# Attention and a gated MLP on one core: q and k of three pairs turned by one DMA transfer each, with two pairs' loads a unit sooner

## The chip, the core and the metric

The kernel runs on one core of a Trainium2 chip. A core has TensorE (PE, matmuls; its weight loads are listed as PEld), VectorE (DVE), ScalarE (ACT), GpSimd (POOL), and SyncE (SP), which here issues DMA transfers. They work side by side and wait for each other through semaphores; each takes its own instructions in order. Sixteen DMA engines move data for the core. The metric is the device time of one execution in microseconds; lower is better.

## The reference

```python
def _attn_ref(q, k, v):                    # q, k, v: (8, 12, 448, 64)
    scores = 1.0 / np.sqrt(64) * np.matmul(q, k.transpose(0, 1, 3, 2))
    m = np.max(scores, axis=-1, keepdims=True)
    e = np.exp(scores - m)
    attn = e / (np.sum(e, axis=-1, keepdims=True) + np.exp(-m) + 1e-09)
    return np.matmul(attn, v)
...
x = attn_out.transpose(0, 2, 1, 3).reshape(3584, 768)
h = x @ w_in                               # (3584, 2048)
sp = np.where(h > 20.0, h, np.log1p(np.exp(np.minimum(h, 20.0))))
return (h * np.tanh(sp)) @ w_out           # (3584, 768), float32
```

All inputs and the output are float32. The output has 3584 rows, 448 for each of eight batches.

## The kernel before, in words

**Pairs and units.** Two heads of a batch make a pair, so there are 48 pairs (p = 0 to 47), six per batch. Their head dimensions of 64 fill TensorE's 128 rows together. Three pairs make a unit (`UNIT_PAIRS`, line 16). Units 0 and 1 are a start-up loop of their own (lines 618 to 651); units 2 to 15 run in the loop of lines 653 to 746, and two more passes (16 and 17) finish the MLP.

**One pair.** q, k and v are loaded as float32 on 112 partitions by SP (`load_pair`, L121, issue at L128), cast to bfloat16 by GpSimd (`cast_pair`, L165, at L179 and L180, and `cast_v`, L188), and q and k are turned, so that the head dimension lies on the partitions. That is done by TensorE: eight transposes of 112 x 128 blocks per pair into a PSUM bank (`transpose_pair`, L208). `evac_qk` then brings them to SBUF: DVE scales q by 1/8 into a block-diagonal tile `qd` (L254, two instructions of 64 rows), and ACT copies k into `kT` (L262). Scores are matmuls of `qd` with `kT` (L311), four steps of up to two 128-row tiles per pair in three PSUM tiles. DVE takes the row maximum (L332), ACT the exponentials with their sums (L345), DVE the denominators (L365, L369), and from pair 12 on DVE divides before the next product (L414, seven per pair, `normalise`). The softmax weights of a pair, 28 blocks of 128 x 128, are turned by one DMA transposing transfer (L422, called a softmax turning here: `eT<-en`, issued by SP). Matmuls with v (`av_pair`, L462) give the turned attention output, which DVE casts into `xT` (L475).

**The MLP.** For a batch that is finished, `mm1_mish` multiplies `xT` by the first weights (L498, six matmuls for each of 16 slices) and ACT applies x * tanh(softplus(x)) (L504). `mm2_part` multiplies by the second weights (L551), DVE copies the result (L534) and SP stores it (L516).

**The order of a unit.** Everything is written out by hand, and each engine's queue has this order. A unit u has two parts. In the first, twelve steps (lines 664 to 717) run the exponentials of u's three pairs, the scores up to three steps ahead, the av products of the pairs of unit u - 1 (from unit 4 on), and mm2 chunks from `plan` as filler on PE. In steps 0, 3 and 6 (`LOAD_AT`, line 592) SP gets the q and k loads of the pair four further on (`LEAD`) and a v load, and GpSimd the casts of q and k three pairs further on. In the second part (lines 724 to 746), eight mm1 slices f = 0 to 7: denominators and the division of u's first pair at f = 0, of the others at f = 3 and 7, each followed by its softmax turning; at f = 1, 3 and 5 the transposes of one pair of the next unit on PE and `evac_qk`; at f = 4, 6 and 7 the first three scores of the next unit.

**Queues and buffers.** SP issues every load, turning and store in the order of the code, and waits in that order. `ld_pool` has three buffers each for q, k and v as loaded; the casted q and k have four buffers each, casted v twelve, `kT` three, `eT` three, and `qd` three (pair p uses p % 3).

Of the kernel before, what the change touches and what calls it, by code (L numbers as in the profile page):

```python
# [10 lines left out]
BF16 = mybir.dt.bfloat16  # L11
# [4 lines left out]
UNIT_PAIRS = 3  # L16
# [3 lines left out]
def kernel(  # L20
# [38 lines left out]
    singles = pool("singles", 1)  # L59
    ld_pool = pool("ld", 3)  # L60
    bf_pool = pool("bf", 4)
    qk_pool = pool("qk", 3)
    st_pool = pool("st", 5)
    hl_pool = pool("hl", 4)
    rb_pool = pool("rb", 2)
# [16 lines left out]
    w_in_sb = singles.tile([128, DM_T, d_ff], BF16)  # L82
    w_out_sb = singles.tile([128, FF_T, d_model], BF16)
    gT = singles.tile([128, FF_T, 2 * S], BF16)

    marks = singles.tile([1, 4, 16], BF16)
    N_EN = 5
# [74 lines left out]
            nc.gpsimd.dma_start(out=dst, in_=src.rearrange("(a p) c -> p a c", p=128))  # L162


    def cast_pair(p, with_v=True):  # L165
        if p >= N_PAIRS:
            return
        q_f, k_f, v_f = (loaded[p].get(nm) for nm in "qkv")
        q_bf = bf_pool.tile([SP_, NT, 2, D], BF16, tag="q_bf", name="q_bf")
        k_bf = bf_pool.tile([SP_, NT, 2, D], BF16, tag="k_bf", name="k_bf")  # L170
        v_bf = bf_pool.tile([SP_, 2, NT * D], BF16, tag="v_bf", name="v_bf", bufs=12)
        by_t = "p h (t d) -> p t h d"
        q_t, k_t = (t.rearrange(by_t, t=NT) for t in (q_f, k_f))
        if p == 0:
            nc.vector.tensor_copy(out=k_bf, in_=k_t)
            for half in (slice(0, NT // 2), slice(NT // 2, NT)):
                nc.vector.tensor_copy(out=q_bf[:, half], in_=q_t[:, half])
        else:
            nc.gpsimd.tensor_copy(out=q_bf, in_=q_t)  # L179
            nc.gpsimd.tensor_copy(out=k_bf, in_=k_t)  # L180
        casted[p] = (q_bf, k_bf, v_bf)
        if with_v:
            cast_v(p)

    def cast_v(p):
        if p >= N_PAIRS:
            return
        nc.gpsimd.tensor_copy(out=casted[p][2], in_=loaded.pop(p)["v"])  # L188

    def transpose_pair(p, bank=None):  # L190
        if p >= N_PAIRS:
            return
        q_bf, k_bf, _ = casted[p]
        if bank is None:
            ps = mo_take()
            ps_k = mo_take() if p == 0 else ps
        else:
            ps, ps_k = sc_tiles[2 - bank][:, 0, :], sc_tiles[2 - bank][:, 1, :]
        by_s = [
            t[:, :].bitcast(BF16).rearrange("p (s n) -> p s n", s=2)[:, s, :]  # L200
            for s, t in enumerate((ps, ps_k))
        ]
        by_2 = sc_tiles[2][:, 0, :].bitcast(BF16)
        srcs = list(enumerate((q_bf, k_bf)))
        for s, src in reversed(srcs) if p == 0 else srcs:
            for t in range(NT):
                to = by_2 if p == 0 and s == 0 and t >= NT // 2 else by_s[s]
                nc.tensor.transpose(  # L208
                    to[:, t * SP_ : (t + 1) * SP_],
                    src[:, t].rearrange("p h d -> p (h d)"),  # L210
                    ident[:SP_, :SP_],
                )
        own = [] if bank is not None else [ps, ps_k] if p == 0 else [ps]
        qkT[p] = (by_s, own)
# [6 lines left out]
    def evac_qk(p, act=False):  # L221
        if p >= N_PAIRS:
            return
        (q_ps, k_ps), own = qkT[p]
        mo_free.extend(own)
        q_reads = []
        qd = q_diag[p % 3]
        kT = qk_pool.tile([128, S], BF16, tag="kT", name="kT")
        if p < DIAG_FROM:
            qT = qd.rearrange("d i h r -> d (i h r)")[:, 0:S]  # L230
            qkT[p] = (qT, kT)
            if p == 0:
                nc.scalar.copy(kT, k_ps[:, 0:S])
                by_2 = sc_tiles[2][:, 0, :].bitcast(BF16)
                for ps, half in (q_ps, slice(0, S // 2)), (by_2, slice(S // 2, S)):
                    nc.vector.tensor_scalar(
                        out=qT[:, half], in0=ps[:, half], scalar1=SCALE, scalar2=None,
                        op0=ALU.mult,
                    )
                return  # L240
            if act:
                nc.scalar.mul(qT, q_ps[:, 0:S], SCALE)
            else:
                q_reads.append(nc.vector.tensor_scalar(
                    out=qT, in0=q_ps[:, 0:S], scalar1=SCALE, scalar2=None, op0=ALU.mult
                ))
        else:
            qkT[p] = (qd, kT)
            if p < DIAG_FROM + 3:
                nc.vector.memset(qd[0:64, :, 1, :], 0.0)  # L250
                nc.vector.memset(qd[64:128, :, 0, :], 0.0)
            for h in range(2):
                rows = slice(64 * h, 64 * h + 64)
                q_reads.append(nc.vector.tensor_scalar(  # L254
                    out=qd[rows, :, h, :],
                    in0=q_ps[rows, 0:S].rearrange("d (i r) -> d i r", i=QB),
                    scalar1=SCALE, scalar2=None, op0=ALU.mult,
                ))
        if own and not act:
            nc.vector.tensor_copy(out=kT, in_=k_ps[:, 0:S])  # L260
        else:
            k_read = nc.scalar.copy(kT, k_ps[:, 0:S])  # L262
            if not own:
                apart(k_read, *q_reads)
# [180 lines left out]
    def av_pair(p, bank=None, beside=None, half=None, hold=False):  # L445
        b, hp = p // HP, p % HP
        eT = att[p]["eT"]
        v_bf = casted[p][2]
        if b not in xT:
            xT[b] = xT_pool.tile([128, DM_T, S], BF16, tag="xT", name="xT")  # L450
        if half is not None:
            bank = free_half(half)
            mms = av_beside.setdefault(half * STEPS + STEPS - 1, [])
        av = mo_take() if bank is None else bank
        for j in range(NT):
            for h in range(2):
                if p >= DIAG_FROM:
                    by_h = eT[0:SP_, j, :].rearrange("c (i h r) -> c h i r", h=2, r=64)
                    e_h = by_h[:, h]
                else:  # L460
                    e_h = eT[0:SP_, j, h * S : (h + 1) * S]
                mm = nc.tensor.matmul(  # L462
                    av[h * 64 : (h + 1) * 64, 0:S],
                    lhsT=v_bf[:, h, j * D : (j + 1) * D],
                    rhs=e_h,
                    start=(j == 0), stop=(j == NT - 1),
                )
                if half is not None:
                    apart(mm, half_max[half])
                    mms.append(mm)  # L470

        def evac():
            to = xT[b][:, hp, :]
            if p >= LATE_DIV:
                read = nc.vector.tensor_copy(out=to, in_=av[:, 0:S])  # L475
            else:
                read = nc.vector.tensor_tensor(
                    out=to, in0=av[:, 0:S], in1=rb.pop(p), op=ALU.mult
                )
            if half in half_exp:  # L480
                apart(read, half_exp[half])
            elif beside is not None or half is not None:
                av_read[beside if half is None else half * STEPS + STEPS - 1] = read
            if bank is None:
                mo_free.append(av)

        if p in spread_copy:
            late.append(spread_copy.pop(p))
        (held if hold else late).append(evac)
        del att[p], casted[p], qkT[p]  # L490
# [100 lines left out]
    LEAD = UNIT_PAIRS + 1  # L591
    LOAD_AT = (0, 3, 6)
    HEAD = HP

    BY_PE = {HEAD - 1: 1, HEAD: -2, HEAD + 1: 2}
    AV_AT = {0: {1: 3, 5: 4, 8: 5}, 1: {1: 8, 4: 6, 8: 7}}
# [5 lines left out]
        load_pair(p, names)  # L602
    keep_busy(8, bank=sc_tiles[0][:, 0, :])
    for p in range(2):
        cast_pair(p, with_v=False)
        transpose_pair(p)
        if p == 0:
            evac_qk(p)
            scores_ahead(3)
    load_pair(3)  # L610
    cast_v(0)
    cast_pair(2, with_v=False)
    cast_v(1)
    cast_v(2)
    load_pair(4)


    for p in range(HEAD):
        for s in range(STEPS):
# [19 lines left out]
            if s == 2:  # L639
                if p >= 3:  # L640
                    spread_rden(p - 3)
                cast_pair(p + 3, with_v=p + 3 < HEAD)
            if s == 3:
                if p >= 3:
                    av_pair(p - 3, hold=True)
# [7 lines left out]
    for u in range(UNITS_PER_B, N_UNITS + 2 * UNITS_PER_B):  # L653
# [5 lines left out]
        p0 = u * UNIT_PAIRS  # L659
        if attn and u >= first_mm2:  # L660
            av_with.update({p0 + i: p0 + i - UNIT_PAIRS for i in range(UNIT_PAIRS)})
        end = min((u + 1) * UNIT_PAIRS, N_PAIRS) * STEPS

        for n in range(steps):
            pi, s = divmod(n, STEPS)
# [20 lines left out]
                fn()  # L686
                done += w
            scores_ahead(end)
            if n in LOAD_AT:
                at = p0 + LOAD_AT.index(n)  # L690
                load_pair(at + LEAD, "qk")
                load_pair(at + 1, "v")
                cast_pair(at + LEAD - 1, with_v=False)
                cast_v(at)
            for pe, n0 in BY_PE.items():
                j = n - n0
                first = 2 if pe == HEAD else 0
# [21 lines left out]

        moe = u < N_UNITS + UNITS_PER_B  # L720
        b, w = (u - UNITS_PER_B) // UNITS_PER_B, u % UNITS_PER_B
        nxt = p0 + UNIT_PAIRS
        todo = sorted(range(p0, nxt), key=lambda p: p in BY_PE)
        for f in range(FF_U):
            if moe:
# [53 lines left out]
```

## Time and profile before

| | |
|---|---|
| median of 3 runs | 480.28 us (480.0 to 481.32) |
| the profiled execution | 479.66 us |
| its span, first to last instruction | 477.9 us |
| granted TensorE clock, mean | 0.996 |
| instructions recorded | 9363 |
| HBM read, written | 45.61 MB, 11.01 MB |

The span is what the views of the profile divide up; the execution takes 1.8 us more than it. In a row of the stretches the numbers are the length in us, the busy us of each engine with its count of instructions, the granted clock, the mean busy share of the DMA engines and the GB/s that they moved. The share adds up the time of all packets, including their waiting, and so can pass 1. In a row of the groups, the part after the bar is the busy time, the mean ns of one instruction, and the engine's idle time just before them with what ended it. In a row of the order of time stand the start, the time to the last one's end, the engine and line, what is done, and how many instructions were merged into the row; for several DMA issues in one row the time includes waits between them.

### The profile page before, as it was taken

How to read it: one execution, taken by the hardware profiler on the slowest of the kernel's cores; microseconds unless marked ns; L12 is line 12 of the kernel's file. 1: busy time of each engine (PE TensorE's matmuls, PEld its weight loads, DVE VectorE, ACT ScalarE, POOL GpSimd, SP SyncE). 2: the span in 40 equal slices, each digit the busy share in tenths (PEclk: the TensorE clock that was granted, in tenths of full speed). 3: DMA queues.
4: the chain of work that ended last, by engine and by line, in shares of the span. 5: the costliest groups of instructions: out<-in, count | busy, mean ns of one | idle time of the engine just before them, and what ended most of it. 6: DMA issues, size and time to landing. Idle time of an engine off the chain costs nothing.

```text
span 477.9 us, 9363 instructions
## 1 busy us (share of the span) xinstructions
PE 458.8 (96%) x3291; PEld 257.8 (54%) x3291; DVE 358.7 (75%) x715; ACT 344.7 (72%) x907; POOL 103.8 (22%) x186
## 2 busy tenths in 40 slices
PE   6878999999999999999999999999999999999996
PEld 3344555555555565556555555555555555556563
DVE  5899849569898998889899979888898889421011
ACT  5998878788797868788787968687887978312300
POOL 3623536106031311304040312204040300000000
PEclk9999999999999999999999999999999999999999
DMA  8999999999999979898989999989989596961122
GB/s 215 227 224 213 234 222 183 185 212 233 195 301 207 261 149 214 211 198 227 192 229 171 267 156 260 198 192 231 190 220 198 173 181 156 156 142 34 34 63 71
DMA packets 204975, 91.09 MB, mean 191 GB/s; under 512 B 161792, under 2 KB 201472, under 8 KB 204928
## 3 DMA queue, kind: packets, MB, share of 16 engines
q1 hardware_dynamic: 197408, 84.18, 81.0%
q0 software_dynamic: 7488, 6.29, 8.8%
q8 instruction: 26, 0.43, 0.4%
q14 instruction: 21, 0.17, 0.1%
q10 hardware_dynamic: 32, 0.02, 0.0%
HBM read 45.61 MB, written 11.01 MB: 118 GB/s over the span
## 4 chain that ended last, share of the span: by engine, by line
PE 69%; DVE 8%; ACT 6%; issue 1%; DVEq 0%
PE mo L498 24%; PE mo L551 24%; PE sc L311 7%; ACT en L345 6%; PE sc L462 6%; DVE negm L332 5%; PE sc L498 3%; PE sc L208 3%; DVE en L414 1%; DVE xT L475 1%; PE mo L462 1%; DVE o_sb L534 1%; PE mo L272 0%; DVE eT L437 0%; ACT L345 0%
## 5 line engine op out<-in xcount | busy, mean ns | idle before, releaser
L345 ACT ACTIVATE en<-sc,negm 128x448 bf16<-128x448 f32 x336 | 208.7, 640 | 22.5 <-DVE negm L332 20.7
L332 DVE TENSOR_REDUCE negm<-sc 128x2 f32<-128x896 f32 x192 | 182.6, 970 | 39.6 <-PE sc L311 29.3
L551 PE MATMUL mo<-w_out_sb,gT 128*128 128x384 bf16 (+1 forms) x1024 | 166.8, 307 | 0.4 <-DVE rb L402 0.4
L498 PE MATMUL mo<-xT,w_in_sb 128*128 128x448 bf16 x672 | 141.9, 353 | 0.3 <-DVE xT L475 0.3
L551 PEld LDWEIGHTS <-gT 128*128 128x128 bf16 x1024 | 96.3, 98 | 56.0 <-issue 1.9
L504 ACT ACTIVATE gT<-mo 128x448 bf16<-128x448 f32 x112 | 59.3, 543 | 78.9 <-PE mo L498 78.6
L498 PEld LDWEIGHTS <-w_in_sb 128*128 128x128 bf16 x768 | 72.7, 98 | 63.4 <-issue 3.2
L179 POOL CAST q_bf<-q_f 112x512 bf16<-112x512 f32 x47 | 29.9, 635 | 222.1 <-DMA q_f<-in_q_dram 196.1
L414 DVE TENSOR_SCALAR en<-en,rden 128x448 bf16<-128x448 bf16 x252 | 74.2, 367 | 0.8
L311 PE MATMUL sc<-kT,qd 128*128 128x448 bf16 x252 | 71.6, 354 | 0.1
L345 ACT ACTIVATION_READ_ACCUMULATOR en<-sc,negm 128x1 f32 x336 | 71.0, 211 | 0.0
L534 DVE COPY o_sb<-mo 128x384 f32<-128x384 f32 (+1 forms) x64 | 31.8, 497 | 48.3 <-PE mo L551 48.1
L462 PE MATMUL sc<-eT,v_bf 112*64 112x448 bf16 x336 | 39.8, 357 | 1.4 <-ACT en L345 0.9
L311 PEld LDWEIGHTS <-qd 128*128 128x128 bf16 x252 | 24.4, 97 | 29.0 <-issue 12.9
L188 POOL CAST v_bf<-v_f 112x512 bf16<-112x512 f32 x48 | 29.9, 624 | 31.5 <-DMA v_f<-in_v_dram 31.4
L254 DVE TENSOR_SCALAR qd<-sc 64x448 bf16<-64x448 bf16 x72 | 27.7, 385 | 6.2 <-PE sc L208 5.4
L462 PEld LDWEIGHTS <-v_bf 112*64 112x64 bf16 x384 | 20.0, 109 | 20.0 <-issue 11.6
L180 POOL CAST k_bf<-k_f 112x512 bf16<-112x512 f32 x47 | 29.2, 622 | 6.1 <-DMA k_f<-in_k_dram 3.5
L262 ACT COPY kT<-sc 128x448 bf16<-128x448 bf16 x39 | 20.8, 534 | 0.6 <-PE sc L208 0.6
L498 PE MATMUL sc<-xT,w_in_sb 128*128 128x448 bf16 x96 | 20.8, 353 | 0.0
L475 DVE CAST xT<-sc 128x448 bf16<-128x448 f32 x33 | 20.3, 614 | 0.0
L208 PEld LDWEIGHTS <-q_bf 112*128 112x128 bf16 x192 | 13.7, 99 | 10.0 <-POOL q_bf L179 2.0
(61 smaller groups left out, 278.9 us busy)
## 6 DMA issues: line engine op xcount, KB each, us to landing
k_f<-in_k_dram SPq DMA_DIRECT2D x48, 224.0 KB, 5.2
q_f<-in_q_dram SPq DMA_DIRECT2D x48, 224.0 KB, 5.2
v_f<-in_v_dram SPq DMA_DIRECT2D x48, 224.0 KB, 5.5
w_in_sb<-in_moe_w_in_dram POOLq DMA_DIRECT2D x12, 256.0 KB, 8.7
w_out_sb<-in_moe_w_out_dram POOLq DMA_DIRECT2D x8, 384.0 KB, 10.1
out_dram<-o_sb SPq DMA_DIRECT2D x7, 336.0 KB, 3.7
out_dram<-o_sb SPq DMA_DIRECT2D x8, 288.0 KB, 4.8
out_dram<-o_sb SPq DMA_DIRECT2D x8, 240.0 KB, 3.4
```

Of the source, the lines that this page charges most:

```text
L179: nc.gpsimd.tensor_copy(out=q_bf, in_=q_t)
L180: nc.gpsimd.tensor_copy(out=k_bf, in_=k_t)
L188: nc.gpsimd.tensor_copy(out=casted[p][2], in_=loaded.pop(p)["v"])
L311: nc.tensor.matmul(sc[:, bk, 0:S], lhsT=qT[:, i].rearrange("d h r -> d (h r)"), rhs=kT, start=True, stop=True,)
L332: half_max[p] = nc.vector.tensor_reduce(out=negm, in_=sc[:, 0 : len(cols), 0:S], axis=AX.X, op=ALU.max, negate=True)
L345: e = nc.scalar.activation(out=st["en"][:, :, c, 0:SP_], in_=sc[:, bk, 0:S].rearrange("q (j c) -> q j c", j=NT), func=AF.Exp, bias=st["neg ...
L414: nc.vector.tensor_scalar(out=en[:, :, i, 0:SP_], in0=en[:, :, i, 0:SP_], scalar1=st["rden"][:, i : i + 1], scalar2=None, op0=ALU.mult,)
L462: mm = nc.tensor.matmul(av[h * 64 : (h + 1) * 64, 0:S], lhsT=v_bf[:, h, j * D : (j + 1) * D], rhs=e_h, start=(j == 0), stop=(j == NT - 1),)
L498: nc.tensor.matmul(h_ps[:, 0:S], lhsT=w_in_sb[:, dm, ff * 128 : (ff + 1) * 128], rhs=xT[b][:, dm, :], start=(dm == 0), stop=(dm == DM_T - 1),)
L504: nc.scalar.activation(out=gT[:, ff, b % 2 * S : b % 2 * S + S], in_=h_ps[:, 0:S], func=AF.Mish)
L534: nc.vector.tensor_copy(out=o_sb[:, cols.start : cols.start + n_dve], in_=st["o"][:, 0:n_dve])
L551: nc.tensor.matmul(st["o"][:, 0:n_cols], lhsT=gT[:, ff, i * 128 : (i + 1) * 128], rhs=w_out_sb[:, ff, cols], start=(ff == 0), stop=(ff == ...
```

## The change

From pair 18 on (`BY_DMA_FROM` = 2 * 6 + 2 * 3) PE no longer turns q and k. GpSimd casts q and k of three pairs into one tile each (`q_cast`, `k_cast`, 112 partitions x 12 blocks x 128 columns), and SP issues two DMA transposing transfers per unit: `k_cast` into `kT_all` (room for six pairs) and `q_cast` into `qT_all` (room for three). `evac_qk` scales q from `qT_all` on DVE as before and no longer copies k. For the pairs before 18 the PE path stays, with `kT` now inside `kT_all` and the casts inside `q_cast` and `k_cast`.

Where things stand changes too. The first turning (pairs 18 to 20) is issued in unit 5 at step 6, behind that step's loads. From unit 6 on all six casts of the next unit's q and k, the two turnings, the q and k loads of one pair and three v loads are put at step 0, behind the softmax turnings of the unit before; the q and k loads of two more pairs are put at step 11, one unit sooner than before, from unit 5 on. The buffers of casted v go from twelve to eight. From unit 5 on k is loaded and cast ahead of q.

In the built program PE has 480 rows fewer (240 transposes, each with its weight load), ACT 30 fewer; DVE has the same number. SP has 20 turnings more.

```diff
-    qk_pool = pool("qk", 3)
+    q_cast, k_cast = (
+        singles.tile([SP_, UNIT_PAIRS, NT, 2, D], BF16, tag=f"{nm}_cast", name=f"{nm}_cast")
+        for nm in "qk"
+    )
+    qT_all = singles.tile([128, UNIT_PAIRS, S], BF16)
+    kT_all = singles.tile([128, 2 * UNIT_PAIRS, S], BF16)
...
+    def turn_by_dma(p):
+        if not BY_DMA_FROM <= p < N_PAIRS:
             return
+        at = p % (2 * UNIT_PAIRS)
+        for to, src in (kT_all[:, at : at + UNIT_PAIRS], k_cast), (qT_all, q_cast):
+            nc.sync.dma_start_transpose(
+                out=to.rearrange("d g (t p) -> d (g t) p", t=NT),
+                in_=src.rearrange("p g t h d -> p (g t h d)"),
+            )
 
     def transpose_pair(p, bank=None):
-        if p >= N_PAIRS:
+        if p >= min(N_PAIRS, BY_DMA_FROM):
             return
...
     def evac_qk(p, act=False):
-        (q_ps, k_ps), own = qkT[p]
+        by_dma = p >= BY_DMA_FROM
+        kT = kT_all[:, p % (2 * UNIT_PAIRS)]
+        (q_ps, k_ps), own = ((qT_all[:, p % UNIT_PAIRS], kT), []) if by_dma else qkT[p]
...
+        if by_dma:
+            return
...
-            if n in LOAD_AT:
+            if n in LOAD_AT and u <= first_mm2 + 1:
                 at = p0 + LOAD_AT.index(n)
-                load_pair(at + LEAD, "qk")
+                names = "qk" if u <= first_mm2 else "kq"
+                load_pair(at + LEAD, names)
                 load_pair(at + 1, "v")
-                cast_pair(at + LEAD - 1, with_v=False)
-                cast_v(at)
+                cast(at + LEAD - 1, names)
+                if n == LOAD_AT[-1]:
+                    turn_by_dma(nxt)
+                cast(at, "v")
+            elif n == 0 and attn:
+                cast(nxt, "kq")
+                cast(p0, "v")
+                for i in range(1, UNIT_PAIRS):
+                    cast(nxt + i, "kq")
+                turn_by_dma(nxt)
+                load_pair(nxt + UNIT_PAIRS, "kq")
+                for i in range(UNIT_PAIRS):
+                    load_pair(p0 + 1 + i, "v")
+                for i in range(1, UNIT_PAIRS):
+                    cast(p0 + i, "v")
+            if n == steps - 1 and u > first_mm2:
+                for i in range(1, UNIT_PAIRS):
+                    load_pair(nxt + UNIT_PAIRS + i, "kq")
```

`cast(p, names)` is the former `cast_pair` and `cast_v` in one; it writes q and k of pair p into place p % 3 of `q_cast` and `k_cast`.

More of the change, by code (lines that the diff above doesn't have):

```diff
@@ L162, in load_w, with cast @@
             nc.gpsimd.dma_start(out=dst, in_=src.rearrange("(a p) c -> p a c", p=128))
-    def cast_pair(p, with_v=True):
+    def cast(p, names):
         if p >= N_PAIRS:
             return
[L168 to L171, printed above, removed]
         by_t = "p h (t d) -> p t h d"
[L173 to L183, printed above, removed]
@@ L185, in cast_v @@
-    def cast_v(p):
-        if p >= N_PAIRS:
-            return
-        nc.gpsimd.tensor_copy(out=casted[p][2], in_=loaded.pop(p)["v"])
+        to = casted.setdefault(p, {})
+        for nm in names:
+            src = loaded[p].pop(nm)
+            if nm != "v":
+                to[nm] = (q_cast if nm == "q" else k_cast)[:, p % UNIT_PAIRS]
+            else:
+                to[nm] = bf_pool.tile([SP_, 2, NT * D], BF16, tag="v_bf", name="v_bf", bufs=8)
+            if nm != "v":
+                src = src.rearrange(by_t, t=NT)
+            if p > 0 or nm == "v":
+                nc.gpsimd.tensor_copy(out=to[nm], in_=src)
+                continue
+            cuts = (0, NT) if nm == "k" else (0, NT // 2, NT)
+            for lo, hi in zip(cuts, cuts[1:]):
+                nc.vector.tensor_copy(out=to[nm][:, lo:hi], in_=src[:, lo:hi])
@@ L190, in transpose_pair @@
+    def turn_by_dma(p):
+        if not BY_DMA_FROM <= p < N_PAIRS:
+            return
+        at = p % (2 * UNIT_PAIRS)
[4 more added lines that the diff above has]
+            )
     def transpose_pair(p, bank=None):
-        if p >= N_PAIRS:
+        if p >= min(N_PAIRS, BY_DMA_FROM):
@@ L192, in transpose_pair @@
             return
-        q_bf, k_bf, _ = casted[p]
+        q_bf, k_bf = (casted[p][nm] for nm in "qk")
         if bank is None:
@@ L227, in evac_qk @@
         qd = q_diag[p % 3]
-        kT = qk_pool.tile([128, S], BF16, tag="kT", name="kT")
         if p < DIAG_FROM:
@@ L447, in av_pair @@
         eT = att[p]["eT"]
-        v_bf = casted[p][2]
+        v_bf = casted[p]["v"]
         if b not in xT:
@@ L593 @@
     HEAD = HP
+    BY_DMA_FROM = 2 * HP + 2 * UNIT_PAIRS
     BY_PE = {HEAD - 1: 1, HEAD: -2, HEAD + 1: 2}
@@ L604 @@
     for p in range(2):
-        cast_pair(p, with_v=False)
+        cast(p, "qk" if p else "kq")
         transpose_pair(p)
@@ L610 @@
     load_pair(3)
[L611 to L614, printed above, removed]
+    cast(0, "v")
+    cast(2, "qk")
+    cast(1, "v")
+    cast(2, "v")
     load_pair(4)
@@ L641 @@
                     spread_rden(p - 3)
-                cast_pair(p + 3, with_v=p + 3 < HEAD)
+                cast(p + 3, "qkv" if p + 3 < HEAD else "qk")
             if s == 3:
@@ L661 @@
             av_with.update({p0 + i: p0 + i - UNIT_PAIRS for i in range(UNIT_PAIRS)})
-        end = min((u + 1) * UNIT_PAIRS, N_PAIRS) * STEPS
+        nxt = p0 + UNIT_PAIRS
+        end = min(nxt, N_PAIRS) * STEPS
         for n in range(steps):
@@ L721 @@
         b, w = (u - UNITS_PER_B) // UNITS_PER_B, u % UNITS_PER_B
-        nxt = p0 + UNIT_PAIRS
         todo = sorted(range(p0, nxt), key=lambda p: p in BY_PE)
```

## The prediction

> **What bounds the kernel now.** I first read the busy shares, then the busy time of each engine unit by unit, then who waits for whom, then the order of one unit engine by engine. A unit is three head pairs; in the steady part one lasts about 26.4 us.
>
> ```profile
> PE 458.8 (96%) x3291; PEld 257.8 (54%) x3291; DVE 358.7 (75%) x715; ACT 344.7 (72%) x907; POOL 103.8 (22%) x186
> ```
>
> ```profile
> 117.70:143.40 25.70, 25.63 (x172) 14.05 (x170) 23.27 (x49) 20.72 (x55) 3.68 (x6) 1.00 1.15 245
> 143.40:169.80 26.40, 26.30 (x182) 15.04 (x181) 23.95 (x49) 21.47 (x56) 7.45 (x12) 1.00 0.93 213
> ...
> 328.00:355.60 27.60, 27.60 (x190) 15.53 (x189) 23.56 (x50) 22.13 (x57) 7.05 (x12) 1.00 0.97 209
> sum 237.90, PE 237.41 PEld 134.03 DVE 209.24 ACT 193.06 POOL 49.67; mean PE 26.38 PEld 14.89 DVE 23.25 ACT 21.45 POOL 5.52
> ```
>
> The stretches run from one unit's first softmax turning to the next one's; the columns are length, then busy time of PE, PEld, DVE, ACT, POOL, then granted clock, DMA share and GB/s. TensorE (PE) has 237.41 of 237.90 us, at full clock; the waits of PE from 143 to 412 us are an empty list. So in these units the time is the sum of PE's own instructions. VectorE (DVE) is second with 23.25 of 26.4. The DMA side, at 0.93 to 0.97, is nearly full too, but nobody on the path waits for it yet.
>
> **The change part by part. 1: 240 transposes leave PE.** One unit's mm1 part, PE in order of time:
>
> ```profile
> 217.98 2.43 PE L498 MATMUL mo<-xT,w_in_sb 128*128 128x448 bf16 x12
> 220.25 0.36 PE L208 MATMUL sc<-ident,q_bf 112*128 112x112 bf16 x4
> 220.45 0.36 PE L208 MATMUL sc<-ident,k_bf 112*128 112x112 bf16 x4
> 220.65 1.30 PE L498 MATMUL sc<-xT,w_in_sb 128*128 128x448 bf16 x6
> ```
>
> A matmul's own duration (0.36 us for four) contains latency that the next one covers; what counts is the distance between starts. Eight transposes of one pair take 220.65 − 220.25 = 0.40 us. Pairs 18 to 47 are 30 pairs, so PE loses 30 × 0.40 = **−12.0 us**, 1.2 us in each of the ten units 5 to 14. PE has no idle time there to swallow it. It is exact if nothing else becomes late; the rest of the working is about that.
>
> **2: what goes with them.** The copy of k out of PSUM leaves ScalarE (ACT), and the scaling of q stays on DVE but reads SBUF.
>
> ```profile
> L262 ACT COPY kT<-sc 128x448 bf16<-128x448 bf16 x39 | 20.8, 534 | 0.6 <-PE sc L208 0.6
> L254 DVE TENSOR_SCALAR qd<-sc 64x448 bf16<-64x448 bf16 x72 | 27.7, 385 | 6.2 <-PE sc L208 5.4
> L414 DVE TENSOR_SCALAR en<-en,rden 128x448 bf16<-128x448 bf16 x252 | 74.2, 367 | 0.8
> L504 ACT ACTIVATE gT<-mo 128x448 bf16<-128x448 f32 x112 | 59.3, 543 | 78.9 <-PE mo L498 78.6
> ```
>
> 30 × 0.534 = 16 us less ACT work stands beside 78.6 us that ACT waits for PE: worth 0. For q from SBUF the nearest row is L414, 0.367 against 0.385 us: 60 × 0.018 = 1 us of DVE, off the path, 0. GpSimd (POOL) has the same nine casts per unit, 5.5 of 26.4 us busy: 0. Should DVE lose its cover, it has 26.4 − 1.2 − 23.25 = 2 us left per unit.
>
> **3: two turnings per unit more in SyncE's (SP's) queue.** SP issues all of this, in order, and an issue holds it:
>
> ```profile
> 196.24 14.65 SPq L422 DMA_TRANSPOSE eT<-en  x3
> 211.00 0.98 SPq L516 DMA_DIRECT2D out_dram<-o_sb  x2
> 212.07 0.49 SPq L128 DMA_DIRECT2D q_f<-in_q_dram  x1
> ...
> 216.31 0.41 SPq L128 DMA_DIRECT2D v_f<-in_v_dram  x1
> 217.17 1.80 SPq L516 DMA_DIRECT2D out_dram<-o_sb  x2
> 222.96 13.80 SPq L422 DMA_TRANSPOSE eT<-en  x3
> ```
>
> ```profile
> L422 SPq DMA_TRANSPOSE eT<-en x30: 4099/4242/5017, 169.9 to 416.9; - x30
> DMA to landing us min/median/max: 6.1/6.5/8.4
> ```
>
> ```profile
> 29.94 4.03 SPq L422 DMA_TRANSPOSE eT<-en  x1
> ```
>
> A softmax turning of 28 blocks of 128 rows holds SP 4.24 us and lands 2.3 us after SP is free. A new turning has 12 blocks of 112 rows, 1344 rows against 3584: in proportion 1.6 us. The row at 29.94 is of 21 blocks (2688 rows) and took 4.03, in proportion 2.0 us; if the time hardly depends on size, it is 4.0. So T, the hold of one new turning, lies between 1.6 and 4.0; I take 2.0, the proportion of the smaller transfer, nearest in size. SP's free time in the unit shown: 14.65 − 3 × 4.24 = 1.9 inside the turnings, 0.45 before 217.17, and 222.96 − 218.97 = 4.0, together 6.3 us. Needed are 2T and the 1.2 us by which the unit shrinks: 5.2 at T = 2.0. It fits, with 1.1 to spare.
>
> The Trainium skill, "Advanced Engine Details and Errata", section "X-Bar Transpose (TRN2)", says that such transfers run about as fast as plain ones, 350 to 400 GB/s. By that a new turning (344 KB) would take an estimated 0.9 us, and the sum below would be −12.0 + 0 + 2.0 = −10.0. The rows disagree: 917,504 bytes in 4.24 us are 216 GB/s.
>
> DMA engines: 213 GB/s over 26.4 us are about 5.6 MB a unit; with 0.69 MB more in 25.2 us they must carry 250 GB/s. In the stretch 117.70:143.40 they carried 245 while PE lost nothing. So it is at the limit of what was seen. A turning that is late first uses up slack: the one issued at 222.96 lands at about 229.3, and PE reads it here:
>
> ```profile
> 232.82 0.88 PE sc L462 x8
> ```
>
> That is 3.5 us later. I put **+2 us** for this: 0.7 us a unit over eight units (6 to 13; from 14 on no q and k are loaded) less the slack, between 0 and the 8 of the second rival.
>
> **4: the first turning, unit 5.** From unit 6 on the new turnings are issued where the loads of 212.07 stand, some 10 us ahead of the first scaling of q in that unit:
>
> ```profile
> 222.82 1.60 DVE L254 TENSOR_SCALAR qd<-sc 64x448 bf16<-64x448 bf16 x4
> ```
>
> So they land in time, also at T = 4.0 (212.1 + 8.0 + 2.3 = 222.4). Unit 5 is different: its turning waits for the cast of pair 20, whose loads go out in the same unit.
>
> ```profile
> 135.40 0.38 SPq L128 DMA_DIRECT2D q_f<-in_q_dram  x1
> 135.88 0.50 SPq L128 DMA_DIRECT2D k_f<-in_k_dram  x1
> 139.44 0.77 SPq L128 DMA_DIRECT2D v_f<-in_v_dram  x1
> 143.44 13.77 SPq L422 DMA_TRANSPOSE eT<-en  x3
> ```
>
> ```profile
> k_f<-in_k_dram SPq DMA_DIRECT2D x48, 224.0 KB, 5.2
> 143.29 1.60 DVE L254 TENSOR_SCALAR qd<-sc 64x448 bf16<-64x448 bf16 x4
> 144.92 0.54 PE L311 MATMUL sc<-kT,qd 128*128 128x448 bf16 x2
> L180 POOL CAST k_bf<-k_f 112x512 bf16<-112x512 f32 x47 | 29.2, 622 | 6.1 <-DMA k_f<-in_k_dram 3.5
> ```
>
> The load at 135.40 lands at 140.6, its cast (0.62 us) ends at 141.2; SP is free by 140.2, so k is turned 141.2 to 143.2, q 143.2 to 145.2, and q lands 2.3 later, at 147.5. DVE stands at it from 143.3, then needs 2 × 0.39, until 148.3. The scores at 144.92, now due at 144.1 without the two pairs' transposes ahead, wait: **+4.2 us** (3.4 at T = 1.6; 8.2 at T = 4.0). Behind that wait stand, on DVE, the normalising of two pairs and, on SP, the four loads issued early and the softmax turnings. They move with PE, so I count them once.
>
> **Sum**, against the profiled execution's own 479.66 us: −12.0 + 2 + 4.2 = −5.8, so 473.9. The median shown, 480.28, is 0.6 above that execution: **474.5 us**.
>
> A hold of 4 us can cost clock. Where PE idled early in the run, the granted clock fell:
>
> ```profile
> 8.00:12.00 4.00, 2.19 (x16) 1.11 (x16) 1.77 (x3) 4.00 (x13) 2.45 (x4) 0.82 1.12 258
> 12.00:17.00 5.00, 4.41 (x26) 1.48 (x25) 3.90 (x6) 4.57 (x14) 2.45 (x4) 0.80 1.13 260
> ```
>
> 4 × 0.18 + 5 × 0.20 = 1.7 us lost. If the hold triggers that once, 476.2; I give this 1 in 4, inside the forecast. The Trainium skill, "TensorE: Matmul & The Clock Gate", section "What's actually happening", has PE fall to half clock after an idle window of some 3.4 us; by that rule the hold is just long enough, and no run here shows it yet.
>
> **The rivals.**
> - *No hold, no lag.* The cast of pair 20 is earlier, or T smaller, and only the −12 is left: 468.3. For it: PE's empty list of waits. Against: in unit 5 even T = 1.6 leaves 3.4 us.
> - *The DMA engines become the bound.* If they carry 235 GB/s, not 250, a unit needs 6.26 MB / 235 = 26.6 us, 1.4 over 25.2; eight units less the slack of 3.5 give 8, and 480.28 − 12 + 8 + 4.2 = 480.5. For it: shares near 0.95. Against: 245 in one stretch.
> - *SP's queue becomes the bound, and the kernel slower.* If a turning's hold hardly shrinks with its size, T = 4.0 and SP needs 8.0 + 1.2 where it has 6.3: 2.9 × 8 − 3.5 = 19.7, with the first hold of 8.2: 480.28 − 12 + 19.7 + 8.2 = 496. It decides from T = 3.1 on, where 8 × 1.1 − 3.5 + 6.4 is 12. For it: 4.03 for 21 blocks against 4.24 for 28. Against: that one ran right behind loads, which can explain its length.
> - *The change does not do what it says.* The order of PE's instructions has 480 rows fewer (240 transposes with their weight loads), so this is out for PE.
>
> **How the numbers follow.** Chances: forecast 0.50 (470 to 478.8), no hold 0.10 (467.5 to 470), DMA engines full 0.20 (478.8 to 484, two thirds of it within 0.3%), SP full 0.20 (484 to 500). The last needs 3.1 of a T between 1.6 and 4.0, hence no more. About 0.3%, 1.4 us, is what a measurement of this kernel can tell from no change. Faster 0.60, same 0.13, slower 0.27. The range 468 to 488 leaves out most of the slower half of the last case and a little at the bottom.
>
> **What would show it.** PE rows L208 fall by 240 and ACT copies of kT by 30. Step 1: units of about 25.2 us after unit 6, PE still without waits. Step 3: the new turnings' hold near 2 us and SP with about 1 us free per unit; if units are longer than 25.2, PE's av matmuls wait for eT, and the DMA share tells engines from SP. Step 4: one PE wait near 144 us of about 4 us, ended by the scaling of q, with DVE waiting for the q turning; perhaps a granted clock below 1.00 behind it. The forecast is wrong if T is over 3 us, or if PE waits in many units.

## The result, and the profile after

| | before | after |
|---|---|---|
| median of six runs each | 480.33 us (478.94 to 481.32) | 475.33 us (472.42 to 480.68) |
| ratio, 95% interval | | 0.989 [0.9868, 0.9911] |
| the profiled execution | 479.66 us | 473.76 us |
| its span | 477.9 us | 472.0 us |
| granted TensorE clock, mean | 0.996 | 0.989 |

The kernel is faster by 1.1%, 5.0 us, where 5.8 were forecast. One run of the changed kernel, the one at 480.68, was disturbed; the ratio leaves it out, the median of six does not (without it, 475.08). The lower mean clock comes from the first 40 us, ahead of everything edited, where the granted clock was 0.87 in this execution and 0.96 in that of before. The busy shares after, and then the chain of work that ended last, first of the kernel before and then of the one after:

```profile
PE 449.1 (95%) x3051; PEld 246.8 (52%) x3051; DVE 365.2 (77%) x715; ACT 332.4 (70%) x877; POOL 103.0 (22%) x186
```

```profile
PE 69%; DVE 8%; ACT 6%; issue 1%; DVEq 0%
```

```profile
PE 46%; DVE 20%; ACT 8%; DMA 6%; SPq 3%; issue 2%; POOL 0%; DVEq 0%; POOLq 0%
```

PE has the 240 transposes less. But DVE has the same 715 instructions and is busy 6.5 us longer, and the chain runs through DVE for 20% of the span instead of 8. The time by unit, in eight stretches from the first softmax turning of unit 6 to that of unit 14 (the columns are those of the stretches of before):

```profile
248.50:274.30 25.80, 24.80 (x155) 13.57 (x154) 24.58 (x49) 19.75 (x53) 4.91 (x9) 1.00 1.01 244
...
sum 204.30, PE 201.72 PEld 110.28 DVE 192.63 ACT 161.88 POOL 43.28; mean PE 25.22 PEld 13.79 DVE 24.08 ACT 20.23 POOL 5.41
```

The units should take 25.2 us. PE's own instructions do (25.22 in the mean), but the unit takes 25.5: PE is idle for 204.30 − 201.72 = 2.6 us, where before it was idle for 0.5 us in nine units. To see in which part of a unit, one can use a mark that the kernel leaves by itself: ACT loads its function table anew at the start of a unit's second part, here the MLP part (L504 before, L518 after), and of its first, the exponential part (L345, L359). Two units, before and then after:

```profile
219.23 1.28 ACT L504 ACT_TABLE_LOAD   x1
229.77 1.28 ACT L345 ACT_TABLE_LOAD   x1
245.99 1.28 ACT L504 ACT_TABLE_LOAD   x1
256.28 1.28 ACT L345 ACT_TABLE_LOAD   x1
272.25 1.28 ACT L504 ACT_TABLE_LOAD   x1
```

```profile
219.24 1.28 ACT L518 ACT_TABLE_LOAD   x1
228.52 1.28 ACT L359 ACT_TABLE_LOAD   x1
244.68 1.28 ACT L518 ACT_TABLE_LOAD   x1
254.20 1.28 ACT L359 ACT_TABLE_LOAD   x1
271.00 1.28 ACT L518 ACT_TABLE_LOAD   x1
```

The MLP part went from 10.54 to 9.28 us (219 to 229) and from 10.29 to 9.52 (245 to 254); 9.16 is the usual length of the second kind. The exponential part in between is as before (16.22, now 16.16), but the one behind it grew from 15.97 to 16.80. Over the whole trace five exponential parts, every second one, grew: 0.48 + 0.31 + 0.83 + 0.75 + 0.56 = 2.9 us, and one MLP part by 0.36. That is the loss to be explained. It does not come from late transfers. PE's waits from 140 to 412 us:

```profile
PE sc L325 <- DVE qd L266: 2.4, 2, 2.2
PE sc L476 <- ACT en L359: 2.4, 5, 0.7
```

The first is, but for 0.2 us, the hold in unit 5. The second has PE waiting for ACT's exponentials; L476, the av product that also needs `eT`, never waits for a transfer. ACT in turn waits for DVE's maxima, and DVE has no free time there. DVE in one such unit, before and then after, with GpSimd's casts in the same stretch after:

```profile
251.69 1.81 DVE L414 TENSOR_SCALAR en<-en,rden 128x448 bf16<-128x448 bf16 x7
...
260.59 0.62 DVE L332 TENSOR_REDUCE negm<-sc 128x1 f32<-128x448 f32 x1 [0.97 <-PE sc L311]
```

```profile
249.97 3.22 DVE L428 TENSOR_SCALAR en<-en,rden 128x448 bf16<-128x448 bf16 x7
...
259.22 0.61 DVE L346 TENSOR_REDUCE negm<-sc 128x1 f32<-128x448 f32 x1
```

```profile
250.10 0.67 POOL L185 CAST k_cast<-k_f 112x512 bf16<-112x512 f32 x1 [1.17 <-DMA k_f<-in_k_dram]
250.72 0.65 POOL L185 CAST q_cast<-q_f 112x512 bf16<-112x512 f32 x1
251.32 0.65 POOL L185 CAST k_cast<-k_f 112x512 bf16<-112x512 f32 x1
251.92 0.65 POOL L185 CAST q_cast<-q_f 112x512 bf16<-112x512 f32 x1
```

The division of the unit's second pair (seven instructions) took 1.81 us before and takes 3.22 now. Four casts that stand one behind the other from 250.10 to 252.57 lie on it. Before, casts fell in this unit on the first division alone, and DVE came to the maximum of 260.59 with 0.97 us to spare. Now that spare time is gone, and ACT waits 0.57 and 0.81 us for maxima behind it:

```profile
259.87 0.63 ACT L359 ACTIVATE en<-sc,negm 128x448 bf16<-128x448 f32 x1 [0.57 <-DVE negm L346]
...
261.40 0.63 ACT L359 ACTIVATE en<-sc,negm 128x448 bf16<-128x448 f32 x1 [0.81 <-DVE negm L346]
```

The second division is slowed in all nine units from 5 to 13 (2.26 to 4.18 us), and not only where time was lost. The unit ahead of this one has an even longer one, 3.57 us, and yet its exponential part did not grow. DVE had 1.37 us to spare there, at the same place, and still has 0.26. Before, and then after:

```profile
234.10 0.62 DVE L332 TENSOR_REDUCE negm<-sc 128x1 f32<-128x448 f32 x1 [1.37 <-PE sc L311]
```

```profile
223.04 3.57 DVE L428 TENSOR_SCALAR en<-en,rden 128x448 bf16<-128x448 bf16 x7
...
232.79 0.62 DVE L346 TENSOR_REDUCE negm<-sc 128x1 f32<-128x448 f32 x1 [0.26 <-PE sc L325]
```

In the units that lost nothing this spare time was 1.37 us before the change, in units 5, 7, 9, 11 and 13, which lost, 0.97 to 1.15. That this decides where the loss falls is read from the rows and was not tested.

The other places that the prediction named: the new turnings, and the softmax turnings of the units from 5 on (issue times in ns, least, median and most), are these:

```profile
L196 SPq DMA_TRANSPOSE kT_all<-k_cast x10: 1278/1588/2687, 139.2 to 365.0; - x10
L196 SPq DMA_TRANSPOSE qT_all<-q_cast x10: 1370/1569/1949, 142.0 to 366.5; - x10
```

```profile
L436 SPq DMA_TRANSPOSE eT<-en x30: 3504/3720/6055, 171.7 to 408.7; - x30
```

So T is 1.6 us, the lower end of the range, and the softmax turnings hold SP for 3.7 us where it was 4.24. The hold of unit 5, on SP, DVE and PE:

```profile
139.18 2.69 SPq L196 DMA_TRANSPOSE kT_all<-k_cast  x1
141.96 1.94 SPq L196 DMA_TRANSPOSE qT_all<-q_cast  x1
```

```profile
146.00 1.58 DVE L266 TENSOR_SCALAR qd<-qT_all 64x448 bf16<-64x448 bf16 x4 [3.38 <-DMA qT_all<-q_cast]
```

```profile
146.83 0.55 PE L325 MATMUL sc<-kT_all,qd 128*128 128x448 bf16 x2 [2.25 <-DVE qd L266]
```

It is where it was expected and of the kind expected, but 2.25 us instead of 4.2. The profiled spans differ by −5.9 us, and the parts add up to it: −11.8 for the transposes (ten MLP parts with the two disturbances taken out), +2.25 hold, +2.9 and +0.36 for the parts above, +0.3 in the start-up, and 0.1 in small pieces.

### The profile page after: what moved, and what is told of

It is laid out like the page before. It is cut to its first block, busy times and chain, and to the rows that moved or that the text cites. A ratio compares the mean times of both kernels' runs of the same rounds, so it can differ in the third digit from the quotient of the medians.

```text
span 472.0 us, 8866 instructions
## 1 busy us (share of the span) xinstructions
PE 449.1 (95%) x3051; PEld 246.8 (52%) x3051; DVE 365.2 (77%) x715; ACT 332.4 (70%) x877; POOL 103.0 (22%) x186
## 4 chain that ended last, share of the span: by engine, by line
PE 46%; DVE 20%; ACT 8%; DMA 6%; SPq 3%; issue 2%; POOL 0%; DVEq 0%; POOLq 0%
PE mo L512 17%; PE mo L565 16%; DVE negm L346 8%; ACT en L359 7%; DVE en L428 7%; PE sc L325 4%; PE sc L476 4%; DMA v_f<-in_v_dram 3%; PE sc L512 2%; DVE qd L266 2%; SPq L196 2%; DMA out_dram<-o_sb 1%; SPq L134 1%; DMA k_f<-in_k_dram 1%; DVE o_sb L548 1%
## 5 line engine op out<-in xcount | busy, mean ns | idle before, releaser
L359 ACT ACTIVATE en<-sc,negm 128x448 bf16<-128x448 f32 x336 | 208.7, 639 | 24.4 <-DVE negm L346 22.6
L512 PE MATMUL mo<-xT,w_in_sb 128*128 128x448 bf16 x672 | 138.6, 352 | 0.3 <-DVE xT L489 0.3
L518 ACT ACTIVATE gT<-mo 128x448 bf16<-128x448 f32 x112 | 59.3, 543 | 82.7 <-PE mo L512 82.5
L512 PEld LDWEIGHTS <-w_in_sb 128*128 128x128 bf16 x768 | 74.2, 98 | 68.8 <-issue 3.2
L428 DVE TENSOR_SCALAR en<-en,rden 128x448 bf16<-128x448 bf16 x252 | 83.4, 403 | 0.9
L325 PE MATMUL sc<-kT_all,qd 128*128 128x448 bf16 x252 | 71.6, 354 | 2.4 <-DVE qd L266 2.4
L359 ACT ACTIVATION_READ_ACCUMULATOR en<-sc,negm 128x1 f32 x336 | 70.7, 210 | 0.0
L476 PE MATMUL sc<-eT,v_bf 112*64 112x448 bf16 x336 | 39.8, 357 | 3.9 <-ACT en L359 3.3
L185 POOL CAST k_cast<-k_f 112x512 bf16<-112x512 f32 x47 | 29.6, 631 | 32.8 <-DMA k_f<-in_k_dram 24.4
L185 POOL CAST q_cast<-q_f 112x512 bf16<-112x512 f32 x47 | 29.6, 629 | 21.4 <-PE sc L325 14.3
L476 PEld LDWEIGHTS <-v_bf 112*64 112x64 bf16 x384 | 20.4, 109 | 22.3 <-issue 14.9
L266 DVE TENSOR_SCALAR qd<-qT_all 64x448 bf16<-64x448 bf16 x60 | 22.6, 377 | 4.1 <-DMA qT_all<-q_cast 3.4
```

The source lines that it names most:

```text
L185: nc.gpsimd.tensor_copy(out=to[nm], in_=src)
L266: q_reads.append(nc.vector.tensor_scalar(out=qd[rows, :, h, :], in0=q_ps[rows, 0:S].rearrange("d (i r) -> d i r", i=QB), scalar1=SCALE, sc ...
L325: nc.tensor.matmul(sc[:, bk, 0:S], lhsT=qT[:, i].rearrange("d h r -> d (h r)"), rhs=kT, start=True, stop=True,)
L359: e = nc.scalar.activation(out=st["en"][:, :, c, 0:SP_], in_=sc[:, bk, 0:S].rearrange("q (j c) -> q j c", j=NT), func=AF.Exp, bias=st["neg ...
L428: nc.vector.tensor_scalar(out=en[:, :, i, 0:SP_], in0=en[:, :, i, 0:SP_], scalar1=st["rden"][:, i : i + 1], scalar2=None, op0=ALU.mult,)
L476: mm = nc.tensor.matmul(av[h * 64 : (h + 1) * 64, 0:S], lhsT=v_bf[:, h, j * D : (j + 1) * D], rhs=e_h, start=(j == 0), stop=(j == NT - 1),)
```

## The experiments

**The theory, and what stands against it.** Theory A: the casts, moved together and no longer spaced out by PE's transposes, fall on DVE's second division, slow it, and that makes the maxima and so the exponentials late. Its rivals leave the casts out of it. Rival B: DVE is late merely because PE's MLP part (called mm1 part in the expectations) is 1.2 us shorter. Rival C: the transfers that the change adds, SP's queue being fuller by two turnings a unit and the DMA engines busier. A third is the moved order of loads and casts as such, whatever they lie beside. A separate question is what the hold in unit 5 costs. The first four kernels ran against 17 runs of the kernel before (median 479.69 us).

**1. The casts wait for the last division.** One GpSimd copy of two values is put ahead of the unit's later casts; it reads the last block of the last pair's divided weights.

```diff
             elif n == 0 and attn:
+                nc.gpsimd.tensor_copy(
+                    out=marks[0:1, 2, 0:2],
+                    in_=att[p0 - 1]["en"][0:1, NT - 1, NTILE - 1, SP_ - 2 : SP_],
+                )
                 cast(nxt, "kq")
```

> The changed kernel, but GpSimd's casts of the next unit's q and k (from unit 6 on) wait for the last division of the unit before, by a copy of two of its values ahead of them. Theory A: after the change the exponential part of every second unit is 0.3 to 0.8 us longer, because casts that fall beside the second division stretch it from 1.81 to over 3.2 us and the maxima behind it come late; over five such units about 2.8 us. With the casts behind the last division those stretches go back to 15.97 us and the time falls from 475.3 to about 472.5 us; the second division takes 1.8 us again. Rival B: DVE is late merely because PE's mm1 part is 1.2 us shorter; the time stays at 475.3. Rival C: SP or the DMA engines are short of time; the later casts hold up the new turnings and the time rises to 476 or more.

Measured: 471.93 us (469.39 to 474.52), ratio 0.9834 [0.9799, 0.9868], 3.4 us below the changed kernel, with intervals that just touch. The six executions form two groups, 469.4 to 470.1 and 473.8 to 474.5, and the median lies between them; so the parts of the unit say more than the total. DVE's divisions and the casts in the unit shown above:

```profile
251.20 1.81 DVE L428 TENSOR_SCALAR en<-en,rden 128x448 bf16<-128x448 bf16 x7
...
260.44 0.62 DVE L346 TENSOR_REDUCE negm<-sc 128x1 f32<-128x448 f32 x1 [1.09 <-PE sc L325]
...
261.51 3.11 DVE L346 TENSOR_REDUCE negm<-sc 128x2 f32<-128x896 f32 x3
```

```profile
259.02 0.17 POOL L715 COPY marks<-en 1x2 bf16<-1x2 bf16 x1 [10.92 <-DVE en L428]
259.15 0.61 POOL L185 CAST k_cast<-k_f 112x512 bf16<-112x512 f32 x1
```

The second division is back at 1.81, the maximum has 1.09 us to spare again, and the exponential parts that had grown are back at 15.97 to 16.05, although the MLP parts are as short as in the changed kernel (9.16 and 9.28). So rival B falls. The casts, and with them the turnings, go out later here, and no PE wait came of it, which is against rival C. The same casts, now from 259 to 263 us, lie beside maxima that read PSUM (three of them take 3.11 us, against 3.08 without casts) and cost nothing. So it is what the casts lie beside that counts. In this execution the hold of unit 5 came out longer:

```profile
148.58 0.93 PE L325 MATMUL sc<-kT_all,qd 128*128 128x448 bf16 x2 [4.48 <-DVE qd L266]
```

```profile
147.00:151.00 4.00, 2.42 (x7) 1.04 (x8) 3.18 (x11) 0.00 (x0) 0.00 (x0) 0.61 0.98 270
```

Here is the predicted size, and the clock that the prediction gave 1 in 4: a granted 0.61 over 4 us behind the wait. The MLP part of unit 5 took 15.08 us, 3.6 more than in the changed kernel's profile; that is why this profiled execution, 473.82 us, is no faster than the changed kernel's, 473.76, although its later units are.

**2. The first turning a unit later.** Pairs 18 to 20 stay on PE, so that no turning has to wait for a fresh load.

```diff
-    BY_DMA_FROM = 2 * HP + 2 * UNIT_PAIRS
+    BY_DMA_FROM = 2 * HP + 3 * UNIT_PAIRS
```

> The changed kernel with DMA turnings from pair 21 instead of 18, so that unit 5 turns on PE and the first turning stands in unit 6 at step 0. If the first turning's hold of PE (2.25 us in the trace) is a cost of its own, it goes, and three pairs' transposes come back (3 x 0.40 = 1.2 us): 475.3 - 2.25 + 1.2 = 474.2 us, with no PE wait near 144 us. If what waits there would have been late anyway (DVE's order in that unit), only the 1.2 come back: 476.5 us.

Measured: 474.27 us (471.43 to 474.86), ratio 0.9869 [0.9847, 0.9892]. The hold is gone (unit 5's MLP part is 10.29 us, as before), and three pairs less give back 1.2 us. The median is the 474.2 of a hold that is a cost of its own; by the medians about 1 us is gained against the changed kernel, with intervals that overlap. The long exponential parts stay, at 16.46 to 16.60. The executions still spread over 3.4 us, so the hold is not all that makes the changed kernel's times spread.

**3. The moves alone.** No pair is turned by DMA; the written order of loads and casts and the buffers are those of the changed kernel.

```diff
-    BY_DMA_FROM = 2 * HP + 2 * UNIT_PAIRS
+    BY_DMA_FROM = N_PAIRS
```

> The changed kernel with no pair turned by DMA (PE turns all 48), so only the new order of loads and casts, the early loads and the smaller buffers of v are left. If the move costs nothing while PE's mm1 part keeps its transposes: 480.3 us, as before. If the crowded casts cost by themselves (every second unit, 0.3 to 0.8 us): 482 to 484 us. If the new order alone brought part of the gain: below 479.

Measured: 479.68 us (478.82 to 484.95), ratio 1.0017 [0.9992, 1.0042]: no difference. All parts have their lengths of before. The casts stand in the same order here, but `q_cast` and `k_cast` are free only when PE has turned the pair in them, and this spaces the casts out as before (a cast of k starts some 0.5 us behind the start of each transposing of k, here those at 248.21, 250.87 and 253.92):

```profile
252.22 1.92 DVE L428 TENSOR_SCALAR en<-en,rden 128x448 bf16<-128x448 bf16 x7
```

```profile
250.87 0.36 PE L219 MATMUL sc<-ident,k_cast 112*128 112x112 bf16 x4
```

```profile
251.36 0.61 POOL L185 CAST k_cast<-k_f 112x512 bf16<-112x512 f32 x1 [0.82 <-POOL v_bf L185]
...
254.40 0.61 POOL L185 CAST k_cast<-k_f 112x512 bf16<-112x512 f32 x1 [1.88 <-issue]
```

The second division keeps its 1.9 us. So the written order alone is not the cause, and the third rival falls; taking PE's transposes away also took away what spaced the casts.

**4. No casts of q and k.** From pair 24 on the casts of q and k are left out (the later pairs work on q and k of pairs 21 to 23); loads and turnings stay.

```diff
-                cast(nxt, "kq")
+                names = "kq" if u == first_mm2 + 2 else ""
+                cast(nxt, names)
...
-                    cast(nxt + i, "kq")
+                    cast(nxt + i, names)
```

> The changed kernel without the casts of q and k from pair 24 on (left out: later pairs use the q and k of pairs 21 to 23; loads and turnings stay). Theory A (casts beside the divisions): the divisions take 1.8 us in nearly all units and the time falls to 472 us or a little below. Rival B (DVE late for the shorter PE part alone): 475.3. Rival C (SP or DMA engines short of time): 475.3 as well, since loads and turnings are unchanged; the two are then still to be told apart.

Measured: 471.26 us (469.52 to 476.5), ratio 0.9837 [0.9799, 0.9875], the same as with waiting casts. The exponential parts that had grown are 16.04 from unit 8 on. Where casts of q and k still lie on a division (unit 6 casts pairs 21 to 23, and the second division ahead of this part takes 3.27 us), the exponential part of 153.83 to 170.61 is 16.78 us long; in the changed kernel the same part was 16.45:

```profile
153.83 1.28 ACT L359 ACT_TABLE_LOAD   x1
170.61 1.28 ACT L518 ACT_TABLE_LOAD   x1
...
205.35 1.28 ACT L359 ACT_TABLE_LOAD   x1
221.39 1.28 ACT L518 ACT_TABLE_LOAD   x1
```

With and without the casts, in one trace: 16.78 and 16.04.

**5. Both edits together.** The copy of run 1 and the later start of run 2. This and the next kernel ran against nine runs of the kernel before (median 479.75 us).

> The two edits of the earlier runs together: GpSimd's casts of the unit wait for the unit's last division, and the first turning is that of pair 21 (27 pairs, issued a unit later, with its loads long landed), so that TensorE has no hold near 144 us. Theory (casts beside the second division were what ate 2.8 us, and the hold is what varies from execution to execution): 479.7 - 27 x 0.40 = 468.9 us, between 468 and 470.5, all executions within about 1 us of each other, the mm1 part of unit 5 at 10.3 us, exponential parts of 16.0 us, no half-clock window between 140 and 160 us. Rival (the two clusters of the run with the waiting casts alone, 469.5 and 474, have nothing to do with the hold): a median near 472 again, executions still spread over 4 us.

Measured: 470.05 us (468.63 to 471.3), ratio 0.9792 [0.9767, 0.9817]. That is the fastest of the versions that compute everything: 5.3 us below the changed kernel and 4.2 below run 2, from which it differs by the copy alone, in both cases with intervals that do not meet. PE's waits from 100 to 412 us:

```profile
PE sc L476 <- ACT en L359: 0.9, 2, 0.6
...
PE sc L325 <- DVE qd L266: 0.2, 1, 0.2
```

The median is 1.1 us above the 468.9 that the sum gives, and its profiled execution lost 1.0 in the start-up, ahead of everything that was edited. The executions lie within 2.7 us, not within 1; what sets the rest of the spread stays open.

**6. No loads of q and k either.** As run 4, and from pair 24 on the q and k loads are left out as well: SP issues six transfers fewer in a unit, and the DMA engines carry 1.3 MB a unit less.

```diff
-                load_pair(nxt + UNIT_PAIRS, "kq")
+                load_pair(nxt + UNIT_PAIRS, "")
...
-                    load_pair(nxt + UNIT_PAIRS + i, "kq")
+                    load_pair(nxt + UNIT_PAIRS + i, "kq" if u == first_mm2 + 1 else "")
```

> As the run without the casts of q and k from pair 24 on, and their q and k loads (48 transfers of 224 KB) are left out too; the turnings stay, and later pairs use q and k of pairs 21 to 23, so the output is not the reference's. It frees SyncE's queue and the DMA engines of about 1.3 MB a unit. Theory (neither SyncE's queue nor the DMA engines set the end of these units): the same time as without the casts, 471 us within 1, and unit parts of 9.2 and 16.0 us. Rival (the transfers are a bound that the casts hid): 468 us or less, with shorter parts in units 6 to 13.

Measured: 469.75 us (469.64 to 473.09), ratio 0.9809 [0.9782, 0.9836]. It overlaps run 4, the fastest executions are alike (469.64 and 469.52), and the unit parts are the same. One stretch of run 4, and the same stretch of this run:

```profile
248.50:274.30 25.80, 25.69 (x161) 14.12 (x160) 23.75 (x49) 20.66 (x55) 3.69 (x6) 1.00 1.09 267
```

```profile
248.50:274.30 25.80, 25.70 (x161) 14.07 (x160) 23.07 (x51) 20.64 (x55) 1.80 (x3) 1.00 0.73 176
```

176 GB/s instead of 267 (over eight units, 190 instead of 242), and PE is busy for the same 25.7 us. The transfers set nothing here. With run 1, which keeps all of them, rival C falls too.

## Why the prediction came out right, and which step of it did not

- **Step 1, −12.0 us: right.** −11.8 in the profile. The distance between starts (0.40 us a pair), not the duration, was the right price.
- **Step 2, the casts at 0: wrong, and this is the step that failed.** It counted GpSimd's casts ("the same nine casts per unit, 5.5 of 26.4 us busy: 0") by their number and asked what waits for them. It did not ask what they lie beside. With PE's transposes gone they close up and fall on a division, and runs 1 and 4 show the price: about 3 us in all. PE was to stay without waits and waited five times for ACT instead, 2.4 us in all. Of the 2 us of free time that DVE was to have left per unit, in every second unit only some 1 us (the 0.97 ahead of the maximum of 260.59) lay where it could cover a slower division.
- **Step 3, +2 us for transfers: wrong in cause.** T is 1.6 and not 2.0 us, SP and the DMA engines had room (run 6), and their lag is 0. The rivals of the full queue (496) and the full engines (480.5) are out. That the sum came near is luck: the casts cost about what was put down for the transfers, and a little more.
- **Step 4, +4.2 us: right in place and chain, too large for this execution.** The k turning began at 139.2, not 141.2, as the load and the cast that it waits for were earlier. The two turnings took 4.7 us and not 4.0, so PE was released 1.5 us earlier than reckoned (146.8, not 148.3), and it came to the wait 0.5 us later (144.6, not 144.1). In four traces (run 4, the changed kernel, run 6, run 1) the hold was 2.10, 2.25, 2.81 and 4.48 us, so 4.2 lies inside what occurs.
- **The clock behind the hold: seen, in one trace.** It fell behind the wait of 4.48 us and not behind those of 2.10, 2.25 and 2.81. That agrees with the Trainium skill, "TensorE: Matmul & The Clock Gate", section "What's actually happening", whose idle window of some 3.4 us lies between them.
- **The time, 474.5 forecast and 475.3 measured:** −11.8 + 2.25 + 3.3 + 0.3, where −12.0 + 4.2 + 2 stood. A hold 2 us too large and 2 us of lag that did not come stand against 3 us on DVE that were missed, and nearly cancel; the −12.0 is the term that the forecast got right by its working.

## What to carry to other kernels

Work that is free by its engine's load can still slow a neighbour that it lies beside: when a change takes away what spaced such work out, ask on which instruction it will fall. Free time in a unit is cover only if it lies between the slowed instruction and the wait behind it. Here one tiny copy that makes the casts wait for the last division is worth 3.4 us by the medians, or 4.2 where the turnings begin a unit later; that later beginning is worth 1 to 2 us, with intervals that overlap.

## What the runs showed of the hardware

- Seven divisions on DVE (SBUF to SBUF, bf16) take 1.81 us alone and 3.22 with four GpSimd casts beside them, and each cast 0.65 instead of 0.61 us; maxima that read PSUM are not slowed (3.11 against 3.08 for three). Over the changed kernel's trace, most slowed divisions grew by about half of the time for which casts lay beside them: the one at 300.32, beside casts almost to its end, took 4.18 us. The Trainium skill, "SBUF — State Buffer", section "SBUF: two separate sides", has a port pair that VectorE's faster modes and GpSimd share under an exclusive lock. Its direction agrees with the rows; the amount, about half, does not follow from it, and that the lock is the mechanism was not tested by itself.
- A transposing transfer of 1344 rows holds SP 1.6 us. That is the proportion of the 4.24 us that a softmax turning of 3584 rows took before; but that one itself went to 3.72 in the changed kernel, whose proportion would be 1.4, and to 3.55 in run 3, where no new turning exists. So it got shorter with the moves of loads, casts and buffers, not with the new turnings; which of the moves does it was not tried.
- The first 113 us hold the same code in the changed kernel and in all six experiments, and yet the third MLP part began at 113.40 us in run 1 and at 116.09 in run 4:

```profile
113.40 1.28 ACT L518 ACT_TABLE_LOAD   x1
```

```profile
116.09 1.28 ACT L518 ACT_TABLE_LOAD   x1
```

These 2.7 us from execution to execution are as large as the terms in dispute, which is why those were read from parts of units and not from totals alone. What sets them is open.
